# A memory-augmented attention and a gated GLU on one core: attention rewritten with transposed scores, packed segments and a fixed TensorE order

## The chip, the core and the metric

The kernel runs on one NeuronCore of a Trainium2 chip. A core has five engines that run their own instruction streams: TensorE (matrix multiply, "PE" in the profile, its weight loads "PEld"), VectorE ("DVE"), ScalarE ("ACT"), GpSimd ("POOL") and SyncE ("SP", which mostly starts transfers). Matmuls write into PSUM, an accumulator memory; [...] large arrays lie in HBM ("dram" in names).

The metric is the device time of one execution in microseconds (us). The span of a profile is the same thing seen by the profiler and is about 1.5 us shorter.

## The reference, cut to what matters

There are 2048 tokens of width 1024, 32 heads of width 128, segments of 32 tokens and 8 memory rows.

```python
xn = layernorm(x)
# A: recurrent attention, one segment after another
mem = mem0                                   # 8 rows
for s in range(64):
    h = concat([mem, xn[32*s : 32*s+32]])    # 40 rows
    q, k, v = h @ Wq, h @ Wk, h @ Wv         # 32 heads of 128
    scores = q @ k.T * 128**-0.5             # causal for tokens; memory rows see everything
    o = (softmax(scores) @ v) @ Wo
    mem = o[:8]                              # feeds the next segment
    out_s = o[8:]
# B: gated GLU on the same xn, F = 3584
y = (sigmoid(xn @ w_gate) * (xn @ w_up)) @ w_down
return x + s * silu(y)
```

Taken literally the 64 segments depend on each other through `mem`. Both kernels avoid that: the 8 memory rows of a later segment are nearly equal (their weights are nearly uniform), so one row per segment stands for all eight. It is found by two rounds of an approximation (mean of v through Wo, twice), and all segments are then computed at once. At the end the kernel recomputes the memory rows, compares them with the approximation, and sets a flag; if the flag were set, an exact sequential version would run. Both kernels have this check and this fallback.

## The kernel before

The stages in their order, with the parts that the change touches.

**1. Normalisation and v.** Each 128-token tile is normalised and transposed on TensorE. Then v is made one block of 512 columns (4 heads) at a time over all 16 token tiles, and a sum of v over each segment:

```python
for cg in range(8):
    for t0 in range(0, NT, TG):                       # TG = 4 tiles to a store
        for tl in range(TG):
            v_ps = psb.tile([P, 512], F32, name="v_ps", tag="big")
            for c in range(KC):                       # KC = 8
                nc.tensor.matmul(v_ps[:], lhsT=xnT[:, c, t*P:(t+1)*P], rhs=wv_sb[:, c, cg*512:(cg+1)*512], ...)
            ...                                       # copy to v_sb on VectorE or ScalarE
            for hh in range(4):
                nc.tensor.matmul(sv_ps[:, hh, 4*t:4*t+4], lhsT=v_sb[:, tl, hh*DH:(hh+1)*DH], rhs=ind4[:], ...)
        nc.gpsimd.dma_start(vx_dram[...], v_sb[:])
```

`xnT` is also stored to HBM in one transfer of 4 MB, for the fallback, on the same queue as the v stores.

**2. Memory rows.** `wo_stage_stream` (o1 through Wo), `vm` (its v), `wo_stage_stream` again, then `vmr` (v of the rows found). Wo is streamed in pieces of 1 MB, each used by 32 matmuls of 64 columns. Gate/up work of the GLU is put between as a filler, in units of 64 matmuls of 512 columns (`filler(2)`, `filler(1)`, ...); there are 28 units in all.

**3. Heads.** Three segments and their three memory rows make a tile of 99 rows (96 tokens, then 3 memory rows), 21 tiles; segment 0 is kept apart (`qt0`, `kt0`, `va0`). For each head:

```python
for (w_, dst, dst0) in ((wq, qt, qt0), (wk, kt, kt0)):
    for (tok0, ntok, bj, bn, first) in blocks:        # 512, 480, 480, 480, 96 tokens
        for c in range(KC):
            nc.tensor.matmul(pr[:, 0:ntok], lhsT=w_[:, c, hh*DH:(hh+1)*DH], rhs=xnT[:, c, tok0:tok0+ntok], ...)
        nc.scalar.copy(dst[...], pr[...])
    for c in range(KC):                               # the memory rows: 72 columns
        nc.tensor.matmul(pm[:, 0:NC], lhsT=w_[:, c, hh*DH:(hh+1)*DH], rhs=cmT[:, c, :], ...)
    ...
for (b0, nb) in batches:                              # 5, 4, 4, 4, 4 tiles
    for j in range(nb):
        nc.tensor.matmul(s_ps[:, j, :], lhsT=qt[:, b0+j, :], rhs=kt[:, b0+j, :], ...)
    pv = softmax_rows(...)     # VectorE: add mask, max, subtract; ScalarE: Exp; VectorE: sum, reciprocal, multiply
    for j in range(nb):
        nc.tensor.transpose(pt_ps[:, j, 0:TR], pv[:, j, :], ident[0:TR, 0:TR])
    nc.scalar.copy(pt[...], pt_ps[...])               # two copies
    for j in range(nb):
        nc.tensor.matmul(o_ps[:, j, :], lhsT=va[:, b0+j, hh*DH:(hh+1)*DH], rhs=pt[:, j, :], ...)
    nc.scalar.copy(otx[...], o_ps[...])               # o is already transposed for the output stage
    nc.vector.tensor_copy(omq[...], o_ps[...])        # memory rows, for the check
while glu_done < ((h + 1) * n_glu_h) // H: filler(1)  # 15 units over 32 heads
```

The framework's scheduler is free to reorder instructions of an engine here, within what dependences allow. After the heads the same is done once for segment 0 of all heads.

**4. The rest of gate/up**, 6 units.

**5. Output.** First the check (`wo_ps`, 256 matmuls of 72 columns, then transposes `tp` and a count), then per 128-token tile:

```python
nc.sync.dma_start(ot[:], oT_dram[:, :, t*P:(t+1)*P])  # o, stored transposed
nc.sync.dma_start(ht[:], hT_dram[t])
for hf in range(2):
    ...  # y_ps: 28 matmuls of 512 columns (down projection), tanh, gate
    ...  # a_ps: 32 matmuls of 512 columns (Wo), multiply, add x
```

PSUM is shared by a pool `psb` of four buffers (tag "big") and smaller pools.

Of the kernel before, what the change touches and what calls it, by code (L numbers as in the profile page):

```python
# [14 lines left out]
PSUM = bass.MemoryType.PSUM  # L15
P = 128
DM = 1024
KC = DM // P
H = 32
# [10 lines left out]
TX = SPT * SEG  # L30
TR = TX + SPT
LN8B = 2.0794415416798357 * (128.0 ** 0.5)
C40 = 0.0250244140625
TAU = 2.0 ** -10
NB = 5


def layernorm_T(tc, x2, xnT, xnT_dram, ident, side=None, extra_dma=None):
    nc = tc.nc
    S = x2.shape[0]  # L40
    NT = S // P
    with ExitStack() as es:
        pool = es.enter_context(tc.tile_pool(name="ln", bufs=1, side=side))
        wk = es.enter_context(tc.tile_pool(name="ln_wk", bufs=3, side=side))
        ps = es.enter_context(tc.tile_pool(name="ln_ps", bufs=2, space=PSUM))
        xall = pool.tile([P, NT, DM], BF16, name="xall")
        for t in range(NT):
            nc.sync.dma_start(xall[:, t, :], x2[t * P:(t + 1) * P, :])
            if extra_dma is not None and t == min(3, NT - 1):
                extra_dma(0)  # L50
        if extra_dma is not None:
            extra_dma(1)
        eps = pool.tile([P, 1], F32, name="eps")
        nc.vector.memset(eps[:], EPS)
        for t in range(NT):
            st = wk.tile([P, 2, 6], F32, name="st")
            for i in range(2):
                nc.vector.bn_stats(st[:, i, :], xall[:, t, i * 512:(i + 1) * 512])
            mv = wk.tile([P, 2], F32, name="mv")
            nc.vector.bn_aggr(mv[:], st[:].rearrange("p a b -> p (a b)"))  # L60
            sd = wk.tile([P, 1], F32, name="sd")
            nc.scalar.activation(sd[:], mv[:, 1:2], ACTF.Sqrt, bias=eps[:])
            rstd = wk.tile([P, 1], F32, name="rstd")
            nc.vector.reciprocal(rstd[:], sd[:])
            xn = wk.tile([P, DM], BF16, name="xn")
            nc.vector.tensor_scalar(xn[:], xall[:, t, :], mv[:, 0:1], rstd[:], op0=ALU.subtract, op1=ALU.mult)
            pt = ps.tile([P, KC, P], BF16, name="pt")
            for c in range(KC):
                nc.tensor.transpose(pt[:, c, :], xn[:, c * P:(c + 1) * P], ident[:])
            nc.scalar.copy(xnT[:, :, t * P:(t + 1) * P], pt[:])  # L70
        nc.gpsimd.dma_start(xnT_dram, xnT[:])


def glu_gate_up_units(tc, wp, sb, xnT, w_gate, w_up, hT_dram, ps, ps_tag, ps_bufs):
    nc = tc.nc
    S = xnT.shape[2]
    TB = min(512, S)
    NTB = S // TB
    TL = TB // P
    for fg in range(FF // 512):  # L80
        wg = wp.tile([P, KC, 512], BF16, name="wg")
        wu = wp.tile([P, KC, 512], BF16, name="wu")
        nc.sync.dma_start(wg[:], w_gate[:, fg * 512:(fg + 1) * 512].rearrange("(c p) n -> p c n", p=P))
        nc.sync.dma_start(wu[:], w_up[:, fg * 512:(fg + 1) * 512].rearrange("(c p) n -> p c n", p=P))
        for tb in range(NTB):
            hst = sb.tile([P, TL, 4, P], BF16, name="hst", bufs=2)
            for fc in range(4):
                g_ps = ps.tile([P, TB], F32, name="g_ps", tag=ps_tag, bufs=ps_bufs)
                for c in range(KC):
                    nc.tensor.matmul(g_ps[:], lhsT=wg[:, c, fc * P:(fc + 1) * P], rhs=xnT[:, c, tb * TB:(tb + 1) * TB],  # L90
                                     start=(c == 0), stop=(c == KC - 1))
                u_ps = ps.tile([P, TB], F32, name="u_ps", tag=ps_tag, bufs=ps_bufs)
                for c in range(KC):
                    nc.tensor.matmul(u_ps[:], lhsT=wu[:, c, fc * P:(fc + 1) * P], rhs=xnT[:, c, tb * TB:(tb + 1) * TB],  # L94
                                     start=(c == 0), stop=(c == KC - 1))
                th = sb.tile([P, TB], F32, name="th")
                nc.scalar.activation(th[:], g_ps[:], ACTF.Tanh, scale=0.5)  # L97
                nc.vector.scalar_tensor_tensor(hst[:, :, fc, :], th[:].rearrange("p (a b) -> p a b", b=P), 1.0,  # L98
                                               u_ps[:].rearrange("p (a b) -> p a b", b=P), op0=ALU.add, op1=ALU.mult)
            nc.sync.dma_start(  # L100
                hT_dram[tb * TL:(tb + 1) * TL, :, fg * 4:(fg + 1) * 4, :].rearrange("t p c j -> p t (c j)"),
                hst[:].rearrange("p t c j -> p t (c j)"))
            yield


def build_mask(nc, maskb):
    nc.gpsimd.memset(maskb[:, 0:TX], 0.0)
    nc.gpsimd.memset(maskb[:, TX:TR], LN8B)

    def sel(region, base, mult, pat, op=ALU.is_ge):  # L110
        nc.gpsimd.affine_select(out=region, in_=region, compare_op=op, fill=NEG, base=base,
                                pattern=pat, channel_multiplier=mult)
    for b in range(SPT):
        xx = maskb[0:TX, b * SEG:(b + 1) * SEG]
        sel(xx, -b * SEG, 1, [[-1, SEG]])
        sel(xx, b * SEG + SEG - 1, -1, [[0, SEG]])
        xm = maskb[0:TX, TX + b:TX + b + 1]
        sel(xm, -b * SEG, 1, [[0, 1]])
        sel(xm, b * SEG + SEG - 1, -1, [[0, 1]])
        sel(maskb[TX:TR, b * SEG:(b + 1) * SEG], -b, 1, [[0, SEG]], ALU.is_equal)  # L120
    sel(maskb[TX:TR, TX:TR], 0, 1, [[-1, SPT]], ALU.is_equal)


def build_mask0(nc, maskb0):
    nc.gpsimd.memset(maskb0[:], 0.0)
    nc.gpsimd.affine_select(out=maskb0[0:SEG, 0:SEG], in_=maskb0[0:SEG, 0:SEG], compare_op=ALU.is_ge, fill=NEG,
                            base=0, pattern=[[-1, SEG]], channel_multiplier=1)


def softmax_rows(nc, sb, s_ps, maskb, R, nb, W, scale, sfx=""):  # L130
    sm = sb.tile([TR, NB, TR], F32, name="sm" + sfx, tag="sm")
    smv = sm[:].rearrange("p a b -> p (a b)")[0:R, 0:nb * W].rearrange("p (a b) -> p a b", b=W)
    nc.vector.tensor_tensor(smv, s_ps, maskb.unsqueeze(1).to_broadcast([R, nb, W]), op=ALU.add)
    mx = sb.tile([TR, 8], F32, name="mx" + sfx, tag="mx")
    nc.vector.tensor_reduce(mx[0:R, 0:nb], smv, axis=AX.X, op=ALU.max)
    nc.vector.tensor_tensor(smv, smv, mx[0:R, 0:nb].unsqueeze(2).to_broadcast([R, nb, W]), op=ALU.subtract)  # L136
    e = sb.tile([TR, NB, TR], F32, name="e" + sfx, tag="e")
    ev = e[:].rearrange("p a b -> p (a b)")[0:R, 0:nb * W].rearrange("p (a b) -> p a b", b=W)
    nc.scalar.activation(ev, smv, ACTF.Exp, scale=scale)  # L139
    ssum = sb.tile([TR, 8], F32, name="ssum" + sfx, tag="ssum")  # L140
    nc.vector.tensor_reduce(ssum[0:R, 0:nb], ev, axis=AX.X, op=ALU.add)
    rs = sb.tile([TR, 8], F32, name="rs" + sfx, tag="rs")
    nc.vector.reciprocal(rs[0:R, 0:nb], ssum[0:R, 0:nb])
    pr_ = sb.tile([TR, NB, TR], BF16, name="pr_" + sfx, tag="pr_")
    pv = pr_[:].rearrange("p a b -> p (a b)")[0:R, 0:nb * W].rearrange("p (a b) -> p a b", b=W)
    nc.vector.tensor_tensor(pv, ev, rs[0:R, 0:nb].unsqueeze(2).to_broadcast([R, nb, W]), op=ALU.mult)
    return pv
# [105 lines left out]
def wo_stage(nc, ps, wo_sb, oT, ncol, tag, bufs):  # L253
    per = min(max(1, 512 // ncol), KC)
    outs = []
    for c0 in range(0, KC, per):
        n = min(per, KC - c0)
        t = ps.tile([P, n, ncol], F32, name="wo_ps", tag=tag, bufs=bufs)
        for ci in range(n):
            c = c0 + ci  # L260
            for h in range(H):
                nc.tensor.matmul(t[:, ci, :], lhsT=wo_sb[:, h, c * P:(c + 1) * P], rhs=oT[:, h, 0:ncol],
                                 start=(h == 0), stop=(h == H - 1))
        outs.append((t, c0, n))
    return outs


def wo_stage_stream(nc, ps, wpool, Wo3, oT, ncol, tag, bufs, dma_eng):
    assert KC * ncol <= 512
    t = ps.tile([P, KC, ncol], F32, name="wos_ps", tag=tag, bufs=bufs)  # L270
    HGS = 4
    for hg in range(H // HGS):
        wo_t = wpool.tile([P, HGS, DM], BF16, name="wo_t")
        dma_eng.dma_start(wo_t[:], Wo3[hg * HGS:(hg + 1) * HGS].rearrange("h e d -> e h d"))
# [372 lines left out]
```

## Time and profile before

| | before |
|---|---|
| time, median of 4 runs | 1744.64 us (1743.32 to 1745.57) |
| span of the profile | 1743.1 us |
| TensorE busy | 1708.4 us, 98% |
| VectorE busy | 704.7 us, 40% |
| ScalarE busy | 538.4 us, 31% |
| HBM traffic | 129.57 MB read, 61.41 MB written |

The stages on TensorE, from its timeline: v from 11.5 us to 265.0, memory rows to 411.4, heads to 1220.8, segment 0 and the rest of gate/up to 1308.1, check to 1322.0, output to 1736.8, end at 1743.1.

How to read it: the page gives for each engine the time in which some instruction of it was running. The "chain that ended last" follows the work back from the last instruction, at each step to what released it. A timeline line has start, length, engine, source line, operation, output and inputs, shape and count, and in brackets the idle time before it and what ended it. A matmul's record covers its whole way through the array, so records of neighbours overlap; the distance between starts is what a matmul costs in a stream.

### The profile page before, as it was taken

How to read it: one execution, taken by the hardware profiler on the slowest of the kernel's cores; microseconds unless marked ns; L12 is line 12 of the kernel's file. 1: busy time of each engine (PE TensorE's matmuls, PEld its weight loads, DVE VectorE, ACT ScalarE, POOL GpSimd, SP SyncE). 2: the span in 40 equal slices, each digit the busy share in tenths (PEclk: the TensorE clock that was granted, in tenths of full speed). 3: DMA queues.
4: the chain of work that ended last, by engine and by line, in shares of the span. 5: the costliest groups of instructions: out<-in, count | busy, mean ns of one | idle time of the engine just before them, and what ended most of it. 6: DMA issues, size and time to landing. Idle time of an engine off the chain costs nothing.

```text
span 1743.1 us, 27616 instructions
## 1 busy us (share of the span) xinstructions
PE 1708.4 (98%) x11673; PEld 853.4 (49%) x11673; DVE 704.7 (40%) x1722; ACT 538.4 (31%) x1231; POOL 37.0 (2%) x72
## 2 busy tenths in 40 slices
PE   7999998999999999999999999999999999999998
PEld 4344444545555555555555555555445444444443
DVE  6121211213755656765676565577312111111111
ACT  6111111113545445554555454555210000000000
POOL 0010010000000000000000000000100000000000
PEclk9999999999999999999999999999999999999999
DMA  9711226354241233222314222410665343343330
GB/s 354 274 68 66 73 73 218 132 164 90 73 134 42 80 84 116 69 83 65 105 61 98 85 73 73 132 39 1 227 237 149 95 125 106 97 115 114 97 107 26
DMA packets 208336, 192.81 MB, mean 111 GB/s; under 512 B 74096, under 2 KB 177568, under 8 KB 208040
## 3 DMA queue, kind: packets, MB, share of 16 engines
q1 hardware_dynamic: 199488, 154.30, 30.0%
q0 software_dynamic: 8720, 36.70, 5.6%
q8 instruction: 93, 1.52, 0.4%
q14 instruction: 35, 0.29, 0.1%
HBM read 129.57 MB, written 61.41 MB: 110 GB/s over the span
## 4 chain that ended last, share of the span: by engine, by line
PE 89%; DMA 4%; DVE 3%; ACT 2%; issue 1%; SPq 0%; ACTq 0%; DVEq 0%
PE pr L477 25%; PE a_ps L596 13%; PE v_ps L366 12%; PE y_ps L588 11%; PE u_ps L94 9%; PE g_ps L90 8%; PE o_ps L504 3%; DMA wo_t<-in_A_Wo_dram 2%; PE s_ps L492 2%; PE pt_ps L496 2%; PE sv_ps L373 1%; PE pm L485 1%; ACT otx L506 1%; PE vmr_ps L415 1%; DMA vx_dram<-v_sb 1%
## 5 line engine op out<-in xcount | busy, mean ns | idle before, releaser
L477 PE MATMUL pr<-xnT,wk 128*128 128x480 bf16 (+2 forms) x1280 | 246.9, 336 | 0.0
L477 PE MATMUL pr<-xnT,wq 128*128 128x480 bf16 (+2 forms) x1280 | 246.4, 336 | 0.0
L366 PE MATMUL v_ps<-wv_sb,xnT 128*128 128x512 bf16 x1024 | 240.9, 379 | 0.0
L90 PE MATMUL g_ps<-xnT,wg 128*128 128x512 bf16 x896 | 234.6, 379 | 0.0
L94 PE MATMUL u_ps<-xnT,wu 128*128 128x512 bf16 x896 | 226.4, 379 | 0.0
L596 PE MATMUL a_ps<-wo_sb,ot 128*128 128x512 bf16 x1024 | 226.2, 379 | 0.0
L588 PE MATMUL y_ps<-wd,ht 128*128 128x512 bf16 x896 | 198.8, 379 | 0.5 <-DMA ht<-hT_dram 0.5
L596 PEld LDWEIGHTS <-ot 128*128 128x128 bf16 x1024 | 100.2, 98 | 120.8
L477 PEld LDWEIGHTS <-wk 128*128 128x128 bf16 x1280 | 109.2, 98 | 87.4
L477 PEld LDWEIGHTS <-wq 128*128 128x128 bf16 x1280 | 108.4, 98 | 88.3
L98 DVE SCALAR_TENSOR_TENSOR hst<-th,u_ps 128x512 bf16<-128x512 f32 x112 | 76.1, 680 | 171.3 <-PE u_ps L94 169.1
L591 ACT ACTIVATE th<-y_ps 128x512 f32<-128x512 f32 x32 | 19.1, 597 | 404.2 <-PE y_ps L588 404.2
L588 PEld LDWEIGHTS <-ht 128*128 128x128 bf16 x896 | 87.5, 98 | 106.1 <-DMA ht<-hT_dram 0.8
L97 ACT ACTIVATE th<-g_ps 128x512 f32<-128x512 f32 x112 | 67.1, 599 | 229.0 <-PE g_ps L90 229.0
L366 PEld LDWEIGHTS <-xnT 128*128 128x128 bf16 x1024 | 90.0, 97 | 89.9 <-issue 0.8
L94 PEld LDWEIGHTS <-wu 128*128 128x128 bf16 x896 | 83.9, 98 | 82.7
L480 ACT CAST qt<-pr 128x480 bf16<-128x480 f32 (+1 forms) x160 | 78.4, 500 | 130.2 <-PE pr L477 130.2
L90 PEld LDWEIGHTS <-wg 128*128 128x128 bf16 x896 | 81.1, 98 | 72.5
L480 ACT CAST kt<-pr 128x480 bf16<-128x480 f32 (+1 forms) x160 | 76.1, 497 | 99.7 <-PE pr L477 99.6
L139 ACT ACTIVATE e<-sm 99x396 f32<-99x396 f32 (+2 forms) x164 | 88.1, 553 | 47.7 <-DVE sm L136 47.7
L369 DVE CAST v_sb<-v_ps 128x512 bf16<-128x512 f32 x56 | 38.7, 692 | 158.3 <-PE v_ps L366 153.3
L371 ACT CAST v_sb<-v_ps 128x512 bf16<-128x512 f32 x72 | 42.1, 585 | 191.5 <-PE v_ps L366 185.7
(591 smaller groups left out, 1502.6 us busy)
## 6 DMA issues: line engine op xcount, KB each, us to landing
vx_dram<-v_sb POOLq DMA_DIRECT2D x32, 512.0 KB, 3.4
wo_t<-in_A_Wo_dram SPq DMA_DIRECT2D x16, 1024.0 KB, 6.7
ot<-oT_dram SPq DMA_DIRECT2D x16, 1024.0 KB, 5.8
va<-vx_dram SPq DMA_DIRECT2D x16, 1008.0 KB, 7.0
oT_dram<-otx SPq DMA_DIRECT2D x16, 1008.0 KB, 8.7
hT_dram<-hst SPq DMA_DIRECT2D x28, 512.0 KB, 2.9
ht<-hT_dram SPq DMA_DIRECT2D x16, 896.0 KB, 5.1
wv_sb<-in_A_Wv_dram SPq DMA_DIRECT2D x8, 1024.0 KB, 13.1
```

Of the source, the lines that this page charges most:

```text
L90: nc.tensor.matmul(g_ps[:], lhsT=wg[:, c, fc * P:(fc + 1) * P], rhs=xnT[:, c, tb * TB:(tb + 1) * TB], start=(c == 0), stop=(c == KC - 1))
L94: nc.tensor.matmul(u_ps[:], lhsT=wu[:, c, fc * P:(fc + 1) * P], rhs=xnT[:, c, tb * TB:(tb + 1) * TB], start=(c == 0), stop=(c == KC - 1))
L97: nc.scalar.activation(th[:], g_ps[:], ACTF.Tanh, scale=0.5)
L98: nc.vector.scalar_tensor_tensor(hst[:, :, fc, :], th[:].rearrange("p (a b) -> p a b", b=P), 1.0, u_ps[:].rearrange("p (a b) -> p a b", b= ...
L139: nc.scalar.activation(ev, smv, ACTF.Exp, scale=scale)
L366: nc.tensor.matmul(v_ps[:], lhsT=xnT[:, c, t * P:(t + 1) * P], rhs=wv_sb[:, c, cg * 512:(cg + 1) * 512], start=(c == 0), stop=(c == KC - 1))
L371: nc.scalar.copy(v_sb[:, tl, :], v_ps[:])
L477: nc.tensor.matmul(pr[:, 0:ntok], lhsT=w_[:, c, hh * DH:(hh + 1) * DH], rhs=xnT[:, c, tok0:tok0 + ntok], start=(c == 0), stop=(c == KC - 1))
L480: nc.scalar.copy(dst[:, bj:bj + bn, 0:TX], pr[:, o:o + bn * TX].rearrange("p (T j) -> p T j", j=TX))
L504: nc.tensor.matmul(o_ps[:, j, :], lhsT=va[:, b0 + j, hh * DH:(hh + 1) * DH], rhs=pt[:, j, :], start=True, stop=True)
L588: nc.tensor.matmul(y_ps[:], lhsT=ht[:, c, :], rhs=wd[:, c, hf * 512:(hf + 1) * 512], start=(c == 0), stop=(c == FC - 1))
L596: nc.tensor.matmul(a_ps[:], lhsT=ot[:, h, :], rhs=wo_sb[:, h, hf * 512:(hf + 1) * 512], start=(h == 0), stop=(h == H - 1))
```

## The change

The change rewrites nearly everything around the big matmuls; what is computed stays the same but for the softmax, which no longer subtracts the row's maximum (the check at the end now also looks at the denominators). Its parts, and what each is for:

1. **Packed segments.** Each segment is laid out with its memory row behind it, 33 rows, in one array `xq` (63 x 33 + 40 = 2119 columns); three segments are 99 neighbouring columns, and segment 0 with the eight rows of `mem0` stands at the end as a 22nd tile. One set of projection matmuls (five blocks of 422 to 425 columns) covers tokens and memory rows. The separate 96- and 72-column matmuls and the epilogue for segment 0 go.
2. **Transposed scores.** `s_ps` is computed as keys x queries, so that its Exp is directly the weight operand of the output matmul. The transposes and their copies go. The mask is multiplied after Exp (a value of 8 stands for the eight memory rows); the denominators come from a column of ones beside v, so an output matmul has 129 columns. Its rows are tokens, not head columns. Weight operands are 128 wide.
3. **A fixed order.** TensorE and SyncE follow the program's order; attention of head h - 1 is placed between the projection blocks of head h.
4. **Smaller, more filler.** Gate/up runs in steps of 16 matmuls of 512 columns (112 in all), 13 of them in the memory stage, 6 in the last attention, 93 after the heads; the heads have none. Wo and w_down are loaded in pieces during these.
5. **Memory stage spread out.** Parts of the first Wo pass are done within the v stage, as soon as the sums of eight heads are there; in the second, vm of one group of heads, a filler step and the Wo part of an earlier group alternate. v is stored after each 128-token tile (256 KB); the `xnT` copy for the fallback goes out in four pieces during the heads.
6. **Output stage.** o is stored as tokens x head columns, and is transposed by the transfer that loads it (four transposing transfers for each 128-token tile, two more for the check's memory rows). The loads are issued one tile ahead. Two `a_ps` groups and the check come before the first use of `ht`.

The core of the diff (cuts are marked with "..."; removed code that is shown above is not repeated):

```diff
+    es_m.enter_context(tc.manual_schedule(engines={PE, SP}))
...
+        for g in range(NG):                      # v, 8 heads at a time; NG = 4
+            sv_ps = ps.tile([P, HPG, NSEG], F32, name="sv_ps", tag="sv", bufs=1)
+            for t in range(NT):
+                v_sb = v_tile(g, t)              # 16 matmuls of 512 columns, two copies, one store
+                if g == 0 and t + 2 < NT:
+                    layernorm(t + 2)
+                if g == 1:
+                    pack(t)                      # xnT -> xq on VectorE
+                if prev is not None:
+                    sv_tile(*prev)               # 8 matmuls of 4 columns, of the tile before
...
+                if pend and t in (6, 10):
+                    hg, o1, h0 = pend[0][:3]
+                    wo_part(acc1, pend[0][3], hg, o1[:, h0:h0 + 4, :])
...
+        for hg in range(H // 4 + 2):
+            if hg < H // 4:
+                wo_t[hg] = wo_load(hg)
+                ...                              # vm_ps, 32 matmuls of 71 columns; o2 on VectorE
+            if hg >= 2:
+                filler(1)
+                wo_part(acc2, wo_t[hg - 2], hg - 2, o2s[hg - 2])
...
+                for i in range(NBLK):            # NBLK = 5
+                    a, b = edges[i], edges[i + 1]
+                    pr = psb.tile([P, 512], F32, name="pr", tag="big")
                     for c in range(KC):
+                        nc.tensor.matmul(pr[:, 0:b - a], lhsT=w_[:, c, hc], rhs=xq[:, c, a:b],
                                          start=(c == 0), stop=(c == KC - 1))
+                    nc.scalar.copy(dst[:, a:b], pr[:, 0:b - a])
+                    yield
+        def s_batch(h, i):
...
+                nc.tensor.matmul(s_ps[:, j * TR:(j + 1) * TR], lhsT=kt[:, o:o + P], rhs=qt[:, o:o + TR], start=True, stop=True)
...
+            nc.scalar.activation(pT[0:TR, o:o + w], s_ps[0:TR, 0:w], ACTF.Exp, scale=scale)
+            nc.vector.tensor_tensor(pv, pv, mask[:].unsqueeze(1).to_broadcast([TR, n, TR]), op=ALU.mult)
...
+        def pv_batch(h, i):                      # three tiles
...
+                    nc.tensor.matmul(o_ps[0:m, j, :], lhsT=pT[0:TR, o:o + m], rhs=va[:, j0 + j, v0:v0 + DH + 1],
+                                     start=True, stop=True)
+            nc.vector.reciprocal(rd, o_ps[0:R, 0:n, d0])
+            nc.vector.tensor_tensor(osb[...], o_ps[0:R, 0:n, e0:e0 + DH], rd.unsqueeze(2).to_broadcast([R, n, DH]), op=ALU.mult)
...
+            plan = [[("s", 0), ("s", 1)], [("s", 2)], [("s", 3)], [("s", 4), ("v", 0)], [("v", 1)], [("v", 2), ("v", 3)],
+                    [("v", 4)], [("v", 5), ("v", 6)], [("v", 7)], []]
...
+        for h in range(H + 1):
+            pj = proj_steps(h) if h < H else None
+            at = attn_steps(h - 1) if h > 0 else None
+            for i in range(2 * NBLK):
+                ...                              # next(pj), next(at): one block, then one step of the plan
...
-    for hg in range(4):
-        nc.gpsimd.dma_start(wo_sb[...], A_Wo[...])
+    for i, _ in enumerate(glu):
+        if i % 4 == 0 and pieces:
+            nc.sync.dma_start(*pieces.pop(0))
...
-            nc.sync.dma_start(ot[:], oT_dram[:, :, t * P:(t + 1) * P])
+            for a in range(4):
+                s = 4 * t + a
+                r0 = X0 if s == 0 else (s - 1) * B1
+                nc.sync.dma_start_transpose(ot[:, :, a * SEG:(a + 1) * SEG], o_dram[r0:r0 + SEG, :])
...
+            if t == 0:
+                outp(t, 0)
+                outp(t, 1)
+                next(chk)                        # wo_ps: 256 matmuls of 80 columns
+                down(t, 0)
```

## The prediction, made before the changed kernel was run

> **What bounds the kernel now.** I read the page first, then the chain of work that ended last, in order of time, and then the timeline of TensorE in each stage.
>
> From the page, the busy time of each engine, the granted clock and the first line of the chain:
>
> ```profile
> PE 1708.4 (98%) x11673; PEld 853.4 (49%) x11673; DVE 704.7 (40%) x1722; ACT 538.4 (31%) x1231; POOL 37.0 (2%) x72
> ...
> PEclk9999999999999999999999999999999999999999
> ...
> PE 89%; DMA 4%; DVE 3%; ACT 2%; issue 1%; SPq 0%; ACTq 0%; DVEq 0%
> ```
>
> TensorE carries the time from end to end at full clock; no other engine is above 40%. But 98% busy doesn't mean that only 2% can be won: a matmul's record (379 ns at 512 columns) is longer than its share of a dense stream, so records overlap and hide short waits. What counts is the distance from start to start. From the chain in order of time (start us, us, what):
>
> ```profile
> 738.99 6.93 PE pr L477 x40
> ...
> 807.29 2.24 PE pr L477 x11
> ...
> 826.07 2.24 PE pr L477 x11
> ...
> 1716.90 6.91 PE a_ps L596 x32
> 1723.81 6.04 PE y_ps L588 x28
> ```
>
> A 512-column matmul costs 6.04 / 28 = 215.7 ns. 40 projection matmuls (8 of 512, 24 of 480, 8 of 96 columns) take 6.93 us, which is exactly columns / 2.4 + 2.5 ns each, even at 96 columns. The two lines at 807.29 and 826.07 are the same place in two successive heads with no gate/up work between them: a head costs 18.78 us.
>
> TensorE's timeline inside that head, and below it the wait on its weight load:
>
> ```profile
> 809.39 0.35 PE L492 MATMUL s_ps<-kt,qt 128*99 128x99 bf16 x4
> 809.58 1.99 PE L477 MATMUL pr<-xnT,wq 128*128 128x480 bf16 x9
> 811.56 0.44 PE L496 MATMUL pt_ps<-ident,pr__9216 99*99 99x99 bf16 x5
> 811.84 0.77 PE L477 MATMUL pr<-xnT,wq 128*128 128x480 bf16 x3
> 812.50 0.47 PE L504 MATMUL o_ps<-pt,va 99*128 99x99 bf16 x5
> 812.81 0.35 PE L496 MATMUL pt_ps<-ident,pr__9251 99*99 99x99 bf16 x4
> ```
> ```profile
> 811.56 0.31 PEld L496 LDWEIGHTS <-pr__9216 99*99 99x99 bf16 x5 [0.47 <-DVE pr__9216 L146]
> ```
>
> Four 99-column matmuls take 809.58 - 809.39 = 0.19 us, 47 ns each. The head's known work is two times (6.93 + 8 x 32.5 ns for the memory columns) = 14.38 us, plus 63 small matmuls (21 scores, 21 transposes, 21 outputs) at 47 ns = 2.96 us: 17.34 us. The other 1.44 us of the 18.78 are waits inside the softmax chain, like the 0.47 us above.
>
> The stage in which the memory rows are approximated (264.9 to 411.4 us), and the start of the output stage:
>
> ```profile
> 274.52 1.11 PE L278 MATMUL wos_ps<-o,wo_t 128*128 128x64 bf16 x32 [0.53 <-DMA wo_t<-in_A_Wo_dram]
> ...
> 278.60 1.11 PE L278 MATMUL wos_ps<-o,wo_t 128*128 128x64 bf16 x32 [1.03 <-DMA wo_t<-in_A_Wo_dram]
> ```
> ```profile
> 1318.02 1.04 PE L563 MATMUL tp<-identf,dd 128*70 128x128 f32 x8 [1.42 <-DMA ot<-oT_dram]
> 1320.37 1.07 PE L563 MATMUL tp<-identf,m 128*70 128x128 f32 x8 [1.31 <-DVE stat L564]
> 1321.98 1.90 PE L588 MATMUL y_ps<-wd,ht 128*128 128x512 bf16 x8 [0.54 <-DMA ht<-hT_dram]
> ```
>
> Here TensorE visibly waits, for streamed weights and for the first tiles of the last stage.
>
> **What the Trainium skill says.** "TensorE: Matmul & The Clock Gate", section "Wait — 56ns, not 53.3ns?", gives N / 2.4 GHz plus about 2.5 ns from start to start when warm; the trace agrees (215.7 ns at 512). It also gives a floor of about 25 ns however narrow; the 4-column sv_ps matmuls stand at about 27.5 ns (0.11 us for four). The same page, "Back-to-back issue gap", says about 81 ns at N = 128 for a stream of load-and-multiply pairs; this trace disagrees (47 ns at 99 columns), and I use the trace. "Weight-path perf modes" there says that the fast weight load needs exactly 128 weights; the change pads the weights of scores and outputs to 128, but since 99-wide weights already run at 47 ns I count no gain from it. "DMA: Bandwidth & Descriptors", section "Latency and other measured facts", gives 261 GB/s for a transposing DMA; no run shows this yet.
>
> **The change part by part.** The number of big matmuls doesn't change: v 1024, gate and up 1792, output 1920, projected columns 64 x 8 x 2119 against 2120. So the gain can only be in small matmuls and waits. By stage, before then after:
>
> *Start, 11.5 us to the first v matmul.* The changed program puts nine bn_stats (0.66 us) ahead of the first normalisation, where the old one has seven, and memory transposes ahead of v: estimate 13.3 us.
>
> *V projection, 253.5 us.* 1024 x 0.2158 = 221.0, 512 sv at 27.5 ns = 14.1, transposes 13 x 0.45 = 5.9, leaving 12.5 us of cold clock (1.1: the first five v matmuls took 2.13 us), waits for a store's buffer (2.8 in one place) and short eviction waits. After: the same 235.1, 14 x 0.45 = 6.3, six of the sixteen Wo groups moved in here (32 x 29.2 ns = 0.93 each, 5.6), cold 1.1, waits 3 (the big xnT store has gone from the store queue; sv comes a whole tile late): 251.1.
>
> *Memory stage, 146.4 us* = 7 gate/up units of 13.81 (96.7) + 16 Wo groups, vm (8.3), vmr (13.8) together 37.0 + 12.7 of waits. After: 13 half-filler steps of 16 x 0.2158 = 3.45 (44.9), ten Wo groups 9.3, vm 8.2, vmr 13.8, waits 3 because a step stands between producer and user: 79.2.
>
> *Heads, 809.5 us* = 15 units (207.2) + 32 x 18.82. After, per head: projections 2 x 8 x (2119 / 2.4 + 5 x 2.5) ns = 14.33; 21 scores at 47 ns and one small = 1.01; no transposes, for the scores are computed transposed; 21 outputs of 129 columns at 129 / 2.4 + 2.5 + 3 = 59 ns and one more = 1.30. Sum 16.63, and I add 0.2 for waits, since attention of one head now lies one head behind the projections: 16.83. ScalarE then has 10 copies at about 0.5 and five Exp at about 0.55, 7.8 us; VectorE eight reciprocals (0.175), eight normalising multiplies (0.55) and five mask multiplies (at most 0.55), 8.5 us: both half of the head. First projection alone 14.3, 31 x 16.83 = 521.7, last attention 2.8, six steps 20.7: 559.5.
>
> *Rest of gate/up, 87.3 us* (6 units and head-0 epilogue of about 4). After: 93 steps x 3.453 = 321.1, no epilogue, 0.5 waits: 321.6. (All 28 units, 112 steps, are 386.7 in both.)
>
> *Output, 13.9 + 414.8 us.* The first is wo_ps (8.4) and 5.5 of waits. After: 256 matmuls of 80 columns at 35.8 ns = 9.2, no wait because two output groups and this check precede the first use of ht; then 414.3; 1 for waits: 424.5. The tail stays at 6.3.
>
> Sum before 1743.2, as the span. Sum after: 13.3 + 251.1 + 79.2 + 559.5 + 321.6 + 424.5 + 6.3 = 1655.5; times stand 1.5 above spans (1744.64 against 1743.1): about 1656 us, 5.1% less. The 88 us come from the heads (63.5: about 40 of waits, 23 of transposes less the wider outputs), the memory stage (15), the epilogue (4), the start of the last stage (4) and the v stage (2.4), less 1.8 at the start.
>
> **The rivals.** (1) *Transposing DMAs become the bound of the last stage.* Each 128-token tile needs 1 MB through four of them in 25.9 us, 40 GB/s. At the skill's 261 GB/s it is 4 us, hidden; the loads are one tile ahead, and those of the first tile can start two gate/up groups earlier. If they ran at 30 GB/s, a tile would take 35 us and the stage 560: 1800 us in all, slower. For it: nothing in the old profile shows such a transfer, and they stand on one queue with the other loads. I give it 6%. (2) *The attention chain keeps its waits.* TensorE now follows the program's order strictly; if a mask multiply or a normalisation on VectorE is late, it can't slip other work in. With the old 1.44 us per head instead of 0.2, heads take 38 us more: 1694. Against it: several microseconds lie between each score batch and its use, and both engines are half idle. (3) *Small matmuls of 129 columns are bound by weight loads* at about 81 ns instead of 59: 15 us more, 1671. (4) *Early waits*: weights, x and stores share the DMA engines, which are full for the first 45 us (335 GB/s over 80 us); with three store buffers v could wait 5 to 10 us more.
>
> **Range and chances.** 1656 supposes nearly no waits. Rivals 2 to 4 in part add up to 20; all small matmuls at their ideal and no waits would give about 1640. Range 1638 to 1680. Faster by over 2% (under 1709.7) unless rival 1 holds or something as large is missed: 0.92. Within 2%: 0.03. Slower: 0.05.
>
> **What would show it.** Right: a head's period between like places of 16.6 to 17.0 us; s_ps and o_ps groups at about 47 and 59 ns a matmul; ScalarE and VectorE at half in the heads; gate/up steps at 3.45 us without gaps; y_ps and a_ps at 25.9 us a tile with no wait on ot; first y_ps without wait. Wrong: waits of TensorE on ot from o_dram in the last stage, or on pT and o_ps in every step; a head period near 18; a first v matmul later than 15 us.

## The result and the profile after

| | before | after |
|---|---|---|
| time, median of 12 and 8 runs | 1745.4 us (1743.32 to 1747.62) | 1656.02 us (1655.48 to 1657.17) |
| span of the profile | 1743.1 us | 1654.3 us |
| TensorE busy | 1708.4 us | 1631.8 us |
| VectorE, ScalarE busy | 704.7, 538.4 us | 464.3, 387.9 us |

The ratio is 0.9488 (95% interval 0.9478 to 0.9497): 5.1% faster, as predicted (1656).

The page of the changed kernel, its busy times, TensorE's granted clock and the first line of the chain that ended last:

```profile
PE 1631.8 (99%) x10444; PEld 845.1 (51%) x10444; DVE 464.3 (28%) x1134; ACT 387.9 (23%) x742; POOL 144.4 (9%) x216
...
PEclk9999999999999999999999999999999999999999
...
PE 98%; DVE 1%; DMA 0%; issue 0%; ACT 0%; SPq 0%; DVEq 0%
```

TensorE's share of the chain rose from 89% to 98%: what other engines and transfers had put into the chain is nearly gone, and TensorE is again at full clock from end to end.

TensorE's timeline of the changed kernel in a head (columns as before: start, length, engine, line, operation, output and inputs, shape, count):

```profile
354.27 1.59 PE L503 MATMUL pr<-xq,wq 128*128 128x422 bf16 x8
355.70 0.58 PE L517 MATMUL s_ps<-qt,kt 128*128 128x99 bf16 x9
356.12 1.60 PE L503 MATMUL pr<-xq,wq 128*128 128x424 bf16 x8
...
364.23 0.51 PE L543 MATMUL o_ps<-va,pT 99*128 99x129 bf16 x6
364.57 1.60 PE L503 MATMUL pr<-xq,wk 128*128 128x424 bf16 x8
...
371.12 0.34 PE L503 MATMUL pr<-xq,wq 128*128 128x422 bf16 x1
```

Nine scores take 356.12 - 355.70 = 0.42 us, 47 ns each; six outputs of 129 columns take 364.57 - 364.23 = 0.34 us, 57 ns each. From 354.27 to 371.12 is one head: 16.85 us, where it was 18.78. No line carries a wait in brackets. VectorE is busy for 7.0 us of this head and ScalarE for 7.2, less than half of it.

The memory stage and the start of the output stage, in the same timeline:

```profile
278.52 1.10 PE L363 MATMUL acc<-o,wo_t 128*128 128x64 bf16 x32
279.45 1.28 PE L426 MATMUL vm_ps<-g1b,wv_sb 128*128 128x71 bf16 x32
280.57 1.89 PE L166 MATMUL g_ps<-xnT,wg 128*128 128x512 bf16 x8
282.30 1.89 PE L170 MATMUL u_ps<-xnT,wu 128*128 128x512 bf16 x8
```
```profile
1223.68 13.98 PE L692 MATMUL a_ps<-wo_sb,ot 128*128 128x512 bf16 x64
1237.50 9.34 PE L634 MATMUL wo_ps<-omT,wo_sb 128*128 128x80 bf16 x256
1246.67 18.30 PE L682 MATMUL y_ps<-wd,ht 128*128 128x512 bf16 x84
```

Each group begins where the one before it has put in its last column; the waits on `wo_t`, `ot` and `ht` that stood in these places are gone.

Read from start to start in TensorE's timeline, stage by stage, against the prediction (us):

| stage | before | predicted | measured |
|---|---|---|---|
| start, to the first v matmul | 11.5 | 13.3 | 15.3 |
| v | 253.5 | 251.1 | 247.6 |
| memory rows | 146.4 | 79.2 | 77.0 |
| heads (before with 15 units of gate/up, after with 6 steps) | 809.5 | 559.5 | 562.6 |
| rest of gate/up | 87.3 | 321.6 | 321.2 |
| check and output | 428.7 | 424.5 | 424.2 |
| tail | 6.3 | 6.3 | 6.4 |

The errors of the rows are +2.0, -3.5, -2.2, +3.1, -0.4, -0.3 and +0.1. They nearly cancel; the hit to the microsecond is luck, while every row within 3.5 us is not.

### The profile page after: what moved, and what is told of

Read it like the earlier page. It is cut to its first block, busy times and chain, and to the rows that moved or that the text cites. A ratio compares the mean times of both kernels' runs of the same rounds, so it can differ in the third digit from the quotient of the medians.

```text
span 1654.3 us, 24526 instructions
## 1 busy us (share of the span) xinstructions
PE 1631.8 (99%) x10444; PEld 845.1 (51%) x10444; DVE 464.3 (28%) x1134; ACT 387.9 (23%) x742; POOL 144.4 (9%) x216
## 4 chain that ended last, share of the span: by engine, by line
PE 98%; DVE 1%; DMA 0%; issue 0%; ACT 0%; SPq 0%; DVEq 0%
PE pr L503 28%; PE v_ps L335 14%; PE a_ps L692 13%; PE g_ps L166 12%; PE y_ps L682 12%; PE u_ps L170 12%; PE o_ps L543 2%; PE s_ps L517 2%; PE acc L363 1%; PE vmr_ps L446 1%; PE sv_ps L352 1%; PE wo_ps L634 1%; PE vm_ps L426 1%; PE pt L314 0%; DMA xq<-in_A_x_dram 0%; PE o_ps L537 0%
## 5 line engine op out<-in xcount | busy, mean ns | idle before, releaser
L503 PE MATMUL pr<-xq,wk 128*128 128x424 bf16 (+2 forms) x1280 | 255.8, 343 | 0.0
L503 PE MATMUL pr<-xq,wq 128*128 128x424 bf16 (+2 forms) x1280 | 255.3, 342 | 0.0
L335 PE MATMUL v_ps<-wv_sb,xnT 128*128 128x512 bf16 x1024 | 232.5, 380 | 0.0
L170 PE MATMUL u_ps<-xnT,wu 128*128 128x512 bf16 x896 | 211.7, 379 | 0.0
L166 PE MATMUL g_ps<-xnT,wg 128*128 128x512 bf16 x896 | 211.7, 379 | 0.0
L503 PEld LDWEIGHTS <-wq 128*128 128x128 bf16 x1280 | 118.3, 97 | 85.3
L547 DVE TENSOR_TENSOR osb<-o_ps,rden 99x384 bf16<-99x384 f32 (+1 forms) x256 | 126.0, 513 | 4.4
L505 ACT CAST kt<-pr 128x424 bf16<-128x424 f32 (+2 forms) x160 | 82.0, 512 | 190.2 <-PE pr L503 187.1
L523 DVE TENSOR_TENSOR pT<-pT,mask 99x396 bf16<-99x396 bf16 (+1 forms) x160 | 59.6, 379 | 194.4 <-ACT pT L521 194.4
L505 ACT CAST qt<-pr 128x424 bf16<-128x424 f32 (+2 forms) x160 | 82.0, 512 | 118.5 <-PE pr L503 117.2
```

The source lines that it names most:

```text
L335: nc.tensor.matmul(v_ps[:], lhsT=xnT[:, c, t * P:(t + 1) * P], rhs=wv_sb[:, c, cg * 512:(cg + 1) * 512], start=(c == 0), stop=(c == KC - 1))
L503: nc.tensor.matmul(pr[:, 0:b - a], lhsT=w_[:, c, hc], rhs=xq[:, c, a:b], start=(c == 0), stop=(c == KC - 1))
L505: nc.scalar.copy(dst[:, a:b], pr[:, 0:b - a])
L523: nc.vector.tensor_tensor(pv, pv, mask[:].unsqueeze(1).to_broadcast([TR, n, TR]), op=ALU.mult)
L547: nc.vector.tensor_tensor(osb[0:R, j0:j0 + n, hh * DH:(hh + 1) * DH], o_ps[0:R, 0:n, e0:e0 + DH], rd.unsqueeze(2).to_broadcast([R, n, DH]) ...
```

## The experiments

In what follows, "after" is the changed kernel. Each run stands beside runs of the kernel before on the same chip.

### Is TensorE dense in the heads, and what does a small matmul cost?

Scores issued twice:

```diff
                 nc.tensor.matmul(s_ps[:, j * TR:(j + 1) * TR], lhsT=kt[:, o:o + P], rhs=qt[:, o:o + TR], start=True, stop=True)
+                nc.tensor.matmul(s_ps[:, j * TR:(j + 1) * TR], lhsT=kt[:, o:o + P], rhs=qt[:, o:o + TR], start=True, stop=True)
```

> The changed kernel with each of the 21 full score matmuls of a head issued twice into the same place (the result does not change). My theory: in the heads TensorE is dense, and each small matmul costs its 47 ns: 21 x 32 x 46.7 ns = 31.4 us more, 1687.5 us. The rival, that the heads still have waits in which such work fits: at most 15 us more. The other rival, that small matmuls cost 81 ns: 54 us more.

Measured: 1686.61 us, 30.6 more than after. From the first projection to the last output matmul, 339.41 to 931.78 us, are 592.4 us, where after has 562.5 (339.90 to 902.35): 29.9 us for 672 added matmuls, 44.5 ns each. That is 0.9 us a head, and all of it shows, so the heads have no waits into which such work would fit. A small matmul costs what the prediction counted for a removed transpose (47 ns), and not the 81 ns of its third rival.

Weights of 99 columns instead of 128:

```diff
-  nc.tensor.matmul(s_ps[:, j * TR:...], lhsT=kt[:, o:o + P], ...)
+  nc.tensor.matmul(s_ps[0:TR, j * TR:...], lhsT=kt[:, o:o + TR], ...)
-                    m = P if o + P <= NP else TR
+                    m = TR
```

> The changed kernel with weight operands of 99 columns in place of 128 for scores and outputs of a head, which is what padding them to 128 avoided. My theory: nothing changes, within 2 us, as 99 wide weights already ran at 47 ns in the kernel before. The rival, that only weights of exactly 128 columns load fast, and a stream of small matmuls is otherwise bound by the load: 21 scores x 32 x (81 - 47) ns = 23 us more, and up to 15 us more for the outputs.

Measured: 1658.02 us, ratio 0.9484 (0.9468 to 0.9500), where after has 0.9488: no difference. From the first projection to the last output matmul are 563.6 us, 1.1 more than after, for 1344 small matmuls. Padding the weights brought nothing here, as was counted. The weight loads themselves did get longer, 126 ns each by their records instead of 98, but in these streams they lie beside the matmuls and cost no time.

### Where did the waits in the heads go?

Attention of head h - 1 as a whole behind the projections of head h, with the same instructions:

```diff
-                if at is not None:
+                if at is not None and pj is None:
                     next(at, None)
+            if at is not None and pj is not None:
+                for _ in at:
+                    pass
```

> The changed kernel with the attention of head h - 1 placed as a whole behind the projections of head h, not one step behind each block. The number of instructions is the same. My theory: the short waits are gone because projections lie between each small step and its use; with nothing between, TensorE follows VectorE, which needs 8 x (0.175 + 0.51) + 5 x 0.38 = 7.4 us a head, against 2.3 us of TensorE work: some 6 us of waits in each of 31 heads, 186 us more, about 1840 us (1780 to 1880). The rival, that the waits went away because transposes, maximum and subtraction went away: at most 45 us more, which is what the old chain lost.

Measured: 1874.14 us, 218 more than after: slower than the kernel before. TensorE's timeline of this run, one head, with the waits in brackets:

```profile
376.54 8.71 PE L503 MATMUL pr<-xq,wq 128*128 128x422 bf16 x40
385.09 7.35 PE L503 MATMUL pr<-xq,wk 128*128 128x422 bf16 x40
392.27 0.58 PE L517 MATMUL s_ps<-qt,kt 128*128 128x99 bf16 x9
393.58 0.73 PE L517 MATMUL s_ps<-qt,kt 128*128 128x99 bf16 x8 [0.73 <-ACT pT L521]
...
396.46 0.97 PE L543 MATMUL o_ps<-va,pT 99*128 99x129 bf16 x6 [1.23 <-DVE osb L547]
397.93 1.10 PE L543 MATMUL o_ps<-va,pT 99*128 99x129 bf16 x6 [0.49 <-DVE rden L546]
...
400.18 1.23 PE L503 MATMUL pr<-xq,wq 128*128 128x422 bf16 x3
```

The attention takes 400.18 - 392.27 = 7.9 us for 2.3 us of matmuls: 5.6 us more, near the 6 expected. The waits in brackets in this head, six with those of the lines left out, make 3.1 of it; the records of matmuls overlap and hide part of the others, and the clock is lower too, 0.76 on the mean of this stretch. What was not expected is the first line: the query projections start 8.55 us before the key projections, which themselves need 7.18, as did the query projections ahead of the first attention of this run (7.19). The granted clock is 0.84 in the 8.6 us behind an attention and 1.00 in the 7.2 after them: it sank over the waits, and that costs another 1.4 us a head. For 31 heads, 31 x (5.6 + 1.4) = 217 us, which is what the run lost. So the placing of attention between the projection blocks is worth 218 us in this design: with neither transposes nor row maximum, the kernel would be slower than before if nothing lay between the steps of its attention.

The kernel before without the row maximum:

```diff
-    nc.vector.tensor_reduce(mx[0:R, 0:nb], smv, axis=AX.X, op=ALU.max)
-    nc.vector.tensor_tensor(smv, smv, mx[...].to_broadcast([R, nb, W]), op=ALU.subtract)
```

> The kernel before, without the row maximum and its subtraction (for these scores the softmax stays the same): the chain from scores to transposes is two VectorE operations shorter, the work of TensorE is the same. My theory: the 1.44 us of waits in a head are the length of the softmax chain, so most of them go: 15 to 45 us less, about 1715 us. The rival, that they come from the single buffers of the transposes and outputs in PSUM and from TensorE's own order: at most 10 us less.

Measured: 1730.0 us, 15.4 less than before, ratio 0.9909 (0.9893 to 0.9924). It is at the lower edge of my theory. Two like places one head apart in TensorE's timeline of this run:

```profile
748.51 0.60 PE L474 MATMUL pr<-xnT,wq 128*128 128x512 bf16 x2
749.03 0.58 PE L489 MATMUL s_ps<-kt,qt 128*99 128x99 bf16 x9
...
766.83 0.60 PE L90 MATMUL g_ps<-xnT,wg 128*128 128x512 bf16 x2
767.35 0.58 PE L489 MATMUL s_ps<-kt,qt 128*99 128x99 bf16 x9
```

A head takes 767.35 - 749.03 = 18.32 us instead of 18.78, and all heads together 793.5 instead of 809.5, so the gain lies there. With two VectorE operations less in the chain, 0.46 of the 1.44 us went that no matmul accounted for. The scheduler also ordered TensorE's matmuls otherwise in this program, so how much of the 0.46 is the shorter chain is not shown. What the remaining 1.0 us is, is only read, not shown: many waits of TensorE's weight loads in the heads name the copy that frees the single buffer of `o_ps`, in this run and in the kernel before (who waited for what, total us, times, longest):

```profile
PEld L501 <- DVE omq L504: 21.8, 66, 0.4
```
```profile
PEld L504 <- DVE omq L507: 18.9, 64, 0.4
```

That is 0.6 to 0.7 us a head, of which matmuls still under way cover a part.

### What is the fixed order worth?

The changed kernel without it, and with it on SyncE alone:

```diff
-    es_m.enter_context(tc.manual_schedule(engines={PE, SP}))          # free_order
+    es_m.enter_context(tc.manual_schedule(engines={SP}))              # sp_order_only
```

> The changed kernel without its fixed order: the scheduler may place TensorE's and SyncE's instructions. On TensorE that changes next to nothing, as the compiled programs show: three places in 10,000 matmuls, of which two are in the last attention and move a group of outputs behind the next gate/up step, where the changed kernel waits 1.2 us twice. On SyncE it moves Wo loads and the copy of xnT for the fallback to earlier places. My theory: the order is not where the gain comes from, the restructuring is; 1653.5 us, within 4 us of the changed kernel (2.4 gained in the last attention, a little lost where the xnT copy or a Wo load stands in front of another). The rival, that the fixed order carries much of the gain: at least 15 us slower.

Measured: 1668.53 us, 12.5 more than after. I had expected less time, so this missed. TensorE's order was indeed the same but for three places; nearly all of the loss is one wait, in TensorE's timeline of this run:

```profile
339.62 1.89 PE L170 MATMUL u_ps<-xnT,wu 128*128 128x512 bf16 x8
352.44 10.29 PE L502 MATMUL pr<-xq,wq 128*128 128x422 bf16 x40 [10.93 <-DMA wq<-in_A_Wq_dram]
```

SyncE's timeline of the same run shows why:

```profile
338.99 0.28 SPq L487 DMA_DIRECT2D va<-vp_dram  x1
339.38 0.30 SPq L486 DMA_DIRECT2D va<-vp_dram  x1
339.72 6.12 SPq L483 DMA_DIRECT2D wq<-in_A_Wq_dram  x1
```

and that of after:

```profile
334.47 0.40 SPq L484 DMA_DIRECT2D wq<-in_A_Wq_dram  x1
335.36 0.39 SPq L485 DMA_DIRECT2D wk<-in_A_Wk_dram  x1
335.80 0.52 SPq L487 DMA_DIRECT2D va<-vp_dram  x1
```

Left free, the scheduler puts loads of v, two of 1 MB (the first at 335.00) and one of 20 KB, ahead of the first query weights, though these wait for nothing; between them stand the last two stores of v, of which the first takes the queue for 3.2 us. The query weights are sent off 5.3 us later than in after (339.72 instead of 334.47), and then share the DMA engines with the 2 MB of v: sending them off takes 6.12 us instead of 0.40, and the DMA engines stay full until they have landed (share 0.85 and 1.13 by the profile, in the two halves of that time).

After the 10.9 us of idleness the 40 matmuls take 10.29 us instead of 7.35, because TensorE's clock has gone down: granted were 0.50 in the first 3.4 us of them, 0.62 in the next 3.5, and then 1.00. "TensorE: Matmul & The Clock Gate" in the Trainium skill, section "What's actually happening", says that the array goes to half clock after an idle window of about 3.4 us, and back after about 3.4 us of sustained work, in windows that run on freely. The half clock agrees. The way back took longer here: the 2.9 us lost are, by estimate, 5.9 us at half clock, more than one such window and less than two.

> The changed kernel with the fixed order on SyncE alone; TensorE's order is the scheduler's, which differs in the memory stage in one place and in the last attention in two. The run with both orders free lost 12.5 us up to the first projection, because three loads of v stood in front of the first query weights on SyncE (TensorE waited 10.9 us for wq and then ran slower for 3 us), and won 2.4 us back in the last attention. My theory: what the fixed order brings is SyncE's; 2.4 us less than the changed kernel, about 1653.5 us (1651 to 1656). The rival, that TensorE's fixed order carries it: at least 8 us more than the changed kernel.

Measured: 1653.85 us, ratio 0.9475 (0.9462 to 0.9488), which overlaps the interval of after; the two waits of 1.2 us in the last attention are absent from its timeline, and its span is 3.3 us shorter than that of after. So the fixed order matters on SyncE; on TensorE it brings nothing, and by the trace costs some 2 us.

### Is the memory stage shorter because of the fillers?

```diff
             if hg >= 2:
-                filler(1)
                 wo_part(acc2, wo_t[hg - 2], hg - 2, o2s[hg - 2])
```

> The changed kernel without the eight gate/up steps that stand between the groups of the second pass through Wo in the memory stage; they run later with the rest of gate/up, so that all work is still done. My theory: these steps hide the Wo loads and VectorE; a group is then 2.0 us of TensorE work, while 1 MB of Wo takes about 3.1 us at the 340 GB/s seen early in the trace: 10 to 25 us more, about 1670 us, and waits of TensorE on wo_t. The rival, that the delay of two groups alone is enough: at most 3 us more.

Measured: 1672.25 us, 16.2 more than after. TensorE's timeline of the second pass:

```profile
293.13 1.89 PE L363 MATMUL acc<-o,wo_t 128*128 128x64 bf16 x32 [3.03 <-DMA wo_t<-in_A_Wo_dram]
296.01 1.89 PE L363 MATMUL acc<-o,wo_t 128*128 128x64 bf16 x32 [1.00 <-DMA wo_t<-in_A_Wo_dram]
300.20 1.89 PE L363 MATMUL acc<-o,wo_t 128*128 128x64 bf16 x32 [2.30 <-DMA wo_t<-in_A_Wo_dram]
```

The waits on `wo_t` add up to 9.5 us in five places, and the last groups take 1.89 instead of 1.10 us, on a lowered clock again. VectorE is waited for once, 0.3 us. So it is the Wo loads that the fillers hide, and nearly them alone; the delay of two groups was enough for VectorE.

### Do the transposing loads cost anything?

Ordinary loads in their place (o then stands untransposed in the operand of the last matmuls, so this run leaves the transposition out):

```diff
-  nc.sync.dma_start_transpose(ot[:, :, a * SEG:(a + 1) * SEG], o_dram[r0:r0 + SEG, :])
+  nc.sync.dma_start(ot[a * SEG:(a + 1) * SEG, :, :].rearrange("p h c -> p (h c)"), o_dram[r0:r0 + SEG, :])
```

> The changed kernel, but with ordinary loads in place of the sixty-four transposing loads of o in the last stage (o then stands untransposed in the operand, so the result is not the reference's; the number of matmuls and the bytes are the same). My theory: the transposing loads are hidden behind TensorE, so nothing changes: within 2 us of 1656. The rival, that transposing loads hold up the last stage somewhere: at least 5 us faster, with the gain between the last gate/up step and the last output tile.

Measured: 1657.0 us, ratio 0.9481 (0.9465 to 0.9497): no change. The loads are hidden. With what margin was asked by two runs that load each piece three times.

```diff
   nc.sync.dma_start_transpose(ot[:, :, a * SEG:(a + 1) * SEG], o_dram[r0:r0 + SEG, :])
+  nc.sync.dma_start_transpose(ot2[:, :, a * SEG:(a + 1) * SEG], o_dram[r0:r0 + SEG, :])
+  nc.sync.dma_start_transpose(ot2[:, :, a * SEG:(a + 1) * SEG], o_dram[r0:r0 + SEG, :])   # in the second run: ox2 and ox3
```

> The changed kernel with every transposing load of o in the last stage issued three times, twice of these into a tile that nobody reads. The DMA engines are busy for about 10.5 us in each tile of 25.9 us of the changed kernel, some 6 to 7 of them with the transposing loads, by estimate. My theory: hidden with a margin, so three times as many (some 24 us of a tile) are at the edge: 0 to 40 us more. The rival, that such loads are slow and only just hidden now: over 100 us more, with TensorE waiting for ot in each of the 16 tiles.

Measured: 1728.68 us, 72 more than after, outside of what either side expected. TensorE waited for `ht`, not for `ot`, 46.3 us in 14 tiles; the rest of the 72 us is about what the lower clock costs (0.985 over the span: 0.015 x 1723.8 = 26 us, an estimate). But SyncE waited too, and for a reason that the experiment itself had made: the third load of a piece wrote the same tile as the second, and so stood until that had landed.

```profile
SPq L612 <- DMA ot<-o_dram: 148.0, 64, 3.9
```

The loads of `ht` stand behind these on the same queue. So this run measures a chain of waits on one queue, and not the rate of the loads. The second run gives the extra loads tiles of their own.

> As the earlier run with every transposing load three times, in which the third load of a piece had to wait for the second, as both wrote the same tile (SyncE waited 148 us for them, 64 times). Here the two extra loads go to two tiles of their own. My theory: the 72 us of that run came from this chain of waits, not from the rate of the loads; now 0 to 15 us more than the changed kernel. The rival, that three transposing loads of 1 MB in 25.9 us are more than the DMA engines can do: at least 40 us more, TensorE waiting for ht or ot in most tiles.

Measured: 1676.72 us, 20.7 more than after, which lies between the 0 to 15 of my theory and the 40 of the rival. Nearly all of it is one wait before the first tile, 18.0 us, and 2.3 us more for the 64 matmuls behind it:

```profile
1241.51 16.24 PE L696 MATMUL a_ps<-wo_sb,ot 128*128 128x512 bf16 x64 [17.95 <-DMA ot<-o_dram]
```

and it is again the experiment's: SyncE held the first load into `ox3`, with everything behind it, until a last store of the gate/up stage had landed (54.2 us, once), probably because `ox3` lies where a buffer of that stage was. From there on there is no wait on `ot` or `ht`. The windows of one tile each, after first, then this run (busy time of each engine in us and how many instructions, then the granted clock, the DMA share and GB/s):

```profile
1301.00:1327.00 26.00, 26.00 (x123) 11.79 (x121) 4.15 (x6) 1.19 (x2) 1.08 (x2) 1.00 0.38 107
```
```profile
1352.00:1378.00 26.00, 26.00 (x122) 11.83 (x121) 4.14 (x6) 1.19 (x2) 1.18 (x3) 1.00 0.78 185
```

The DMA share goes from 0.38 to 0.78 with 2 MB more: 0.40 x 26 / 2 = 5.2 us of all DMA engines for 1 MB, so some 200 GB/s by estimate. The prediction had reckoned with 261; the measurement decides, and even at 200 the loads of the changed kernel need a fifth of a tile's time.

### A version that is faster than both

Three small edits to after, at places that its profile names:

```diff
-        load_x(0); load_wv(0, 0, 4); load_x(1); ...          # wv on ScalarE's queue, at once
+        load_x(0); load_x(1); ...; load_x(2); load_x(3)
+        load_wv(0, 0, 8, nc.sync); load_x(4); load_wv(1, 0, 8, nc.sync)
-  [("v", 5), ("v", 6)], [("v", 7)], []]
+  [("v", 5), ("v", 6)], [], [("v", 7)]]
-                if pj is None and i in (0, 1, 2, 3, 5, 7):
+                if pj is None:
                     filler(1)
```

> The changed kernel with three small edits: the first four tiles of x are loaded ahead of the v weights, all on one queue, as in the kernel before (start: 3 us less); the last output group of a head, which waits about 0.2 us for VectorE, goes into the empty last step (31 x 0.2 = 6 us less); in the last attention a gate/up step follows every step (2.4 us less). My theory: 11 us less, about 1645 us (1643 to 1650). The rival, that these waits are covered by something that comes later: within 3 us of the changed kernel.

Measured: 1649.71 us, at the upper end of what was expected, ratio 0.9449 (0.9436 to 0.9462), 6.3 us less than after, and faster than both kernels. Two of the three edits did what was expected: the first v matmul comes at 12.30 us instead of 15.32, and the last attention has no wait on `osb`. The third did nothing: a head still takes 16.84 us. In after the wait was put down to VectorE; here VectorE's last multiply ended at 602.78, 1.7 us ahead, and the time is still there. The weight loads of the two kernels, after first (in brackets the idle time and its releaser):

```profile
605.39 0.09 PEld L537 LDWEIGHTS <-pT 40*40 40x40 bf16 x1 [0.35 <-DVE osb L547]
```
```profile
604.46 0.09 PEld L538 LDWEIGHTS <-pT 40*40 40x40 bf16 x1 [0.35 <-issue]
```

So VectorE was not the cause. This matmul differs from its neighbours in that its weights have 40 rows and 40 columns, and the next run changes the rows.

```diff
-  nc.tensor.matmul(o_ps[0:L, 0, :], lhsT=pT[0:L, X0:NP], rhs=va[0:L, NTL, v0:v0 + DH + 1], ...)
+  nc.tensor.matmul(o_ps[0:L, 0, :], lhsT=pT[0:TR, X0:NP], rhs=va[:, NTL, v0:v0 + DH + 1], ...)   # rows 40 to 98 of va are zero
```

> The tidied kernel, with the last output matmul of a head (40 rows of weights, 40 columns) computed over all 99 rows: rows 40 to 98 of v and of its column of ones are zero there, so the result does not change. In the tidied kernel this matmul still has 0.35 us ahead of its weight load, though nothing is waited for, and 0.26 us from the end of the block before it to the start of the next, where 0.06 would do. My theory: a weight load of fewer rows than those of the matmuls around it is not taken ahead of time; with 99 rows it is, 0.2 us x 32 = 6.4 us less than the tidied kernel, about 1643.5 us. The rival, that the 40 columns or the single matmul cause it: within 1.5 us of the tidied kernel.

Measured: 1650.06 us: no difference from the tidied kernel. The same place of this run:

```profile
603.63 0.10 PEld L541 LDWEIGHTS <-pT 99*40 99x40 bf16 x1 [0.35 <-issue]
```

So few rows are not needed for it: 40 columns are enough. The kernel before has the same gap where 40-column weights follow full ones, in the scores of its segment 0, and also where weights have 40 rows and all 128 columns, in the outputs there:

```profile
1221.32 1.04 PE L90 MATMUL g_ps<-xnT,wg 128*128 128x512 bf16 x4
1222.29 0.37 PE L517 MATMUL s_ps<-kt,qt 128*40 128x40 bf16 x8
...
1226.92 0.82 PE L90 MATMUL g_ps<-xnT,wg 128*128 128x512 bf16 x3
1227.67 0.37 PE L526 MATMUL o_ps<-pt,va 40*128 40x40 bf16 x8
```

Four matmuls of 215.7 ns end their stream at 1222.18, three at 1227.57; the next starts 0.11 and 0.10 later. Either a small number of rows or of columns thus brings the gap. Weights of 99 columns don't show it in the run above that has them. "TensorEngine Tiling (Array Packing)" in the Trainium skill, section "Key Properties", says that "Changing tiling mode (not just tile) drains the TensorE", and the modes that its section "Available Configurations" lists have tiles of 64 or 32 rows or columns; 40 would fit such a tile and 99 would not. That agrees with all the places here, but whether these matmuls change the mode no run shows, and a run with this operand widened past 64 in both was not made, so the cause stays open.

## Why the prediction was right, point by point

*Heads (63.5 us of the gain; measured 60.4).* Right in mechanism and nearly in size. 16.85 us a head against 16.83; scores at 47 and outputs at 57 ns against 47 and 59; projections 14.37 against 14.33. The 0.2 us that I had added "for waits" is there, but as something else: it is the narrow matmul (40 x 40 weights) at the end of a head, not a late engine. The term that was mis-sized is the last attention, 25.9 us from its first scores to its end where I had 23.5: I overlooked that three output groups follow each other without a gate/up step between, twice, and that with only two `o_ps` buffers the third waits for VectorE, 1.2 us each time.

*"The other 1.44 us are waits inside the softmax chain."* Not shown: the run with a chain shorter by two operations, and with another order, won 0.46. That these waits disappear in the changed kernel is shown, and that without independent work between its steps the new attention would wait 5.6 us a head; that the old 1.44 were all the chain's length is not.

*Memory stage (15 us).* Right; 77.0 against 79.2. Two terms were mis-sized: of the 3 us for waits none came within the stage, and `vm` took 9.0 us instead of 8.2 (96 of its matmuls from 271.71 to 275.07, 35 ns each). The run without fillers shows the mechanism, with the Wo loads as what is hidden, where I had written "between producer and user".

*Start (-1.8 us).* Too small: it is -3.8, and with 15.3 us one of the signs of being wrong, a first v matmul later than 15 us, came true. I had counted the bn_stats and not the transfers. In the chain of waits of the changed kernel the first long piece is the load of x, 6.8 us, where the kernel before has 2.8 (start, length, what):

```profile
2.15 6.82 DMA xq<-in_A_x_dram
```

The v weights, 2 MB sent off at once on ScalarE's queue, share the DMA engines with the first x tiles. The tidied kernel, with x ahead of them, starts v 3.0 us earlier.

*v stage (2.4 us).* It gained 5.9. The mis-sized term is again the waits, which I took for 3 us: TensorE waits once, 0.6 us, at the end of the stage. That the smaller stores did it was not tried.

*Output (4 us) and rest of gate/up.* Right to 0.4 us.

*The rivals.* Transposing loads as the bound: not so; after the first tile three times as many were hidden too. Waits in the attention chain: absent, and the run without interleaving shows what they would have cost, 218 us where the rival had 38. 129-column matmuls at 81 ns: not so, 57. Early waits: in part, 2 us at the start.

## What to carry to other kernels

On an engine that is nearly always busy, look for what still stands in its way between the big matmuls, and put independent work between a small step and the one that uses its result: here that alone decided between 1656 and 1874 us. When loads share a queue, what is needed first and waits for nothing goes first. And before a named releaser is believed, see whether it had long been done: a wait that stays when its supposed cause is moved away belongs to something else.

## What was not expected of the hardware

- Short waits cost twice: with single waits of at most 1.23 us, in an attention that took 7.9 us for 2.3 us of matmuls, the granted clock of TensorE sank to 0.86 on the mean of a head, and the next 40 matmuls took 8.55 us instead of 7.18.
- A matmul whose weights have 40 columns, between others of 128, costs some 0.2 us more than its 129 columns would, with 40 rows as with 99; about half of it lies ahead of it and half behind.
- A transposing load of 32 x 4096 holds SyncE's queue for 1.26 to 1.34 us in most cases, so four of them in a row take 5.6 us to start; a load behind them is that much later.
